# A reloaded tile that lands in the place of its own second norm: adaLN attention and token mixer on one Trainium2 core

## The chip, the cores and the metric

The kernel runs on one core of a Trainium2 chip. Its engines are TensorE (PE in the profile), VectorE (DVE), ScalarE (ACT), GpSimd (POOL) and SyncE (SP), which here issues all DMAs, in the order in which they stand in its queue. Every engine works through its own instructions in order and waits for the others by semaphores.

The metric is the device time of the whole program in microseconds (us). Each line of the profile's views that begins with a time gives it in us from the start of the span.

## The reference

Sequence length 2048, width 1024, 32 heads, 3584 hidden units of the mixer. Cut to what matters here:

```python
x = A_x
mod = (_silu(c) @ w_mod).reshape(c.shape[0], 6, 1, -1)
sa, ca, ga, sb, cb, gb = (mod[:, i] for i in range(6))
h = _layernorm(x) * (1 + ca) + sa
x = x + ga * _A_ref(h, wq, wk, wv, wo, beta)     # attention with memory, then @ wo
h = _layernorm(x) * (1 + cb) + sb                # first norm of the stage below, modulated
x = x + gb * _B_ref(h, w1, b1, w2, b2)           # _B_ref begins with h = _layernorm(h): the second norm
```

`_B_ref` is an MLP over the tokens: second layer norm, `w1` (tokens to 3584), gelu, `w2` back, transposed. So after the attention's output projection each token passes through two layer norms in a row, with a modulation between them, before the token MLP.

## The kernel before

The program has three stages: attention (projections, scores, values, to about 1060 us), the output projection with the two norms (989 to 1213 us, its beginning interleaved with the last heads of the attention), and the token MLP in two large products (from 1214 us to the end). The change lies in the middle stage.

The 2048 tokens are 16 tiles of 128. `product(tt)` (L711) makes the attention's output for one tile: it loads the head outputs (`otr`, L714), splits them into a high and a low part (`ots`; ACT casts, DVE subtracts), loads the tile's rows of x (`x1`, L718), and runs 48 matmuls, 24 for each half of the columns, into a PSUM bank of the tag `pj`, which has two. DVE evicts each half by adding it to x and summing the row (L732). The sum, x1, is stored to `x1d` (L734), since it is needed again much later.

`out_proj(tt)` (L739) then returns three functions. `modulated` (L750) computes the mean, has ACT square the whole tile for the variance (`rstd`, L699; the square is L703, its small operations L705 to L709), and makes two passes on DVE: L754, out of x1 into h2, and L755, in place on h2. `normed` (L757) is the second norm: mean (L759), square on ACT (L703 again, of h2), small operations, and one pass on ACT in place (L762). `paired` (L764) keeps h2 of tiles 0 to 7; when tile k+8 is done, it forms with tile k the seven operands of a Strassen-like product: combinations by DVE (L688 to L691), then for k under 3 seven splits into the tiles `bA` (ACT casts, DVE subtracts, L122 and L125), and for other k stores to `hcd` (L777 to L779).

The order of the tiles is 0, 1, 8, 2, 9, 3, 10, 4, 11, 5, 12, 6, 13, 7, 14, 15. There is one exception: after tile 1 the products of tiles 2 and 3 (`EARLY`) are made at once, while the attention still runs, without their norms. So the products' order is 0, 1, 2, 3, 8, 9, 10, 4, 11, 5, ... When tiles 2 and 3 come up in the order, their x1 is loaded again from `x1d` (L744) and only the norms are made.

Places in SBUF come from pools by tag. `x1` has two places (512 KB each); all sixteen x1 and, before the change, both reloads share them in the order in which they are asked for. `h2` has three. A tile that asks for a place waits, by semaphores, until the last reader of the tile before it in that place is done. A scheduler orders each engine's instructions when the program is built; nothing is ordered by hand around the change, and a different pool use gives a different order on each engine.

When the stage ends, its pools are closed and the first product of the token MLP begins: `prepare` (L798) loads a unit of `w1` (L803) and splits it into seven operands `sp` (casts by ACT, L122), `load_b` (L855) loads the pairs stored in `hcd` back (L858), and `mix` (L828) runs the matmuls (L843).

Of the kernel before, what the change touches and what calls it, by code (L numbers as in the profile page):

```python
# [7 lines left out]
F32 = mybir.dt.float32  # L8
# [9 lines left out]
S, D, H, DH, F = 2048, 1024, 32, 32, 3584  # L18
P = 128
# [27 lines left out]
def attention_and_mlp(ctx, tc, x, wq, wkv, wo, beta, w1, b1, w2, b2, c, wm_a, wm_b, out):  # L47
    nc = tc.nc
    V, A, G, T, SY = nc.vector, nc.scalar, nc.gpsimd, nc.tensor, nc.sync
# [4 lines left out]
    x1d = dram.tile([NT, P, D], F32, name="x1d")  # L54
# [63 lines left out]
    def split(dst, src, hi_eng, lo_eng):  # L118

        hi, lo = dst[:, 0], dst[:, 1]  # L120
        if hi_eng is A:
            A.copy(hi, src)  # L122
        else:
            hi_eng.tensor_copy(hi, src)
        lo_eng.tensor_tensor(lo, src, hi.bitcast(F32), op=ALU.subtract)  # L125
# [541 lines left out]
    w = cw_pool.__enter__()  # L667
# [18 lines left out]
    def t_combos(E, b11, b12, b21, b22, t):  # L686

        E.tensor_tensor(t[:, 0], b12, b11, op=ALU.subtract)  # L688
        E.tensor_tensor(t[:, 1], b22, t[:, 0], op=ALU.subtract)
        E.tensor_tensor(b12, b22, b12, op=ALU.subtract)  # L690
        E.tensor_tensor(t[:, 2], b21, t[:, 1], op=ALU.subtract)  # L691
# [7 lines left out]
    def rstd(src, nm, mv, sq):  # L699

        if sq is None:
            sq = wq_.tile([P, D], BF16, tag="sq", bufs=1, name="sq")
        A.activation(sq, src, AF.Square, bias=nm, accum_out=mv[:, 2:3])  # L703
        v, r0, t = mv[:, 0:1], mv[:, 1:2], mv[:, 2:3]
        A.activation(r0, t, AF.Ln, scale=1.0 / D, bias=eps)  # L705
        A.activation(r0, r0, AF.Exp, scale=-0.5)
        V.tensor_scalar(v, t, -0.5 / D, -0.5 * EPS, op0=ALU.mult, op1=ALU.add)
        V.tensor_scalar(t, v, r0, r0, op0=ALU.mult, op1=ALU.mult)
        V.tensor_scalar(r0, t, 1.5, r0, op0=ALU.add, op1=ALU.mult)  # L709

    def product(tt):  # L711

        r = wr_.tile([P, NK, P], F32, tag="otr", bufs=1, name=f"otr{tt}")
        SY.dma_start(r, oT[:, :, P * tt:P * tt + P].rearrange("g p n -> p g n"))  # L714
        os_ = ws_.tile([P, 2, D], F32R, tag="ots", bufs=2, name=f"ots{tt}")
        split(os_, r.rearrange("p a b -> p (a b)"), A, V)
        x1 = w.tile([P, D], F32, tag="x1", bufs=2, name=f"x1_{tt}")
        SY.dma_start(x1, x[P * tt:P * tt + P])  # L718
        ma = w.tile([P, 8], F32, tag="ma", bufs=2 + len(EARLY), name=f"ma{tt}")
        if tt == 0:  # L720
            for i in range(1, 3):
                gm[i] = w.tile([P, D], F32, name=f"gm{i}")
                spread(gm[i], i)
        for nh in range(2):
            ps = bank("pj", 2, f"po{tt}_{nh}")
            n = 0
            for ct in range(NK):
                for i, j in ((0, 0), (0, 1), (1, 0)):
                    T.matmul(ps, os_[:, i, P * ct:P * ct + P], wop[ct, nh][:, j], start=(n == 0), stop=(n == 3 * NK - 1))  # L729
                    n += 1  # L730
            c0, c1 = 512 * nh, 512 * nh + 512
            V.scalar_tensor_tensor(x1[:, c0:c1], ps, 1.0, x1[:, c0:c1], op0=ALU.mult, op1=ALU.add,  # L732
                                   accum_out=ma[:, 5 + nh:6 + nh])
        SY.dma_start(x1d[tt], x1)  # L734
        return x1, ma

    done = {}

    def out_proj(tt):  # L739

        if tt in done:
            ma = done[tt]
            x1 = w.tile([P, D], F32, tag="x1", bufs=2, name=f"x1r_{tt}")
            SY.dma_start(x1, x1d[tt])  # L744
        else:
            x1, ma = product(tt)
        h2 = w.tile([P, D], F32, tag="h2", bufs=3, name=f"h2_{tt}")
        mb = w.tile([P, 8], F32, tag="mb", bufs=2, name=f"mb{tt}")

        def modulated():  # L750
            nm = ma[:, 4:5]
            V.tensor_scalar(nm, ma[:, 5:6], ma[:, 6:7], -1.0 / D, op0=ALU.add, op1=ALU.mult)
            rstd(x1, nm, ma, h2 if tt == 15 else None)
            V.scalar_tensor_tensor(h2, x1, nm, gm[2], op0=ALU.add, op1=ALU.mult)  # L754
            V.scalar_tensor_tensor(h2, h2, ma[:, 1:2], gm[1], op0=ALU.mult, op1=ALU.add, accum_out=mb[:, 5:6])  # L755

        def normed():  # L757
            nm = mb[:, 4:5]
            V.tensor_scalar_mul(nm, mb[:, 5:6], -1.0 / D)  # L759
            rstd(h2, nm, mb, x1 if tt == 15 else None)  # L760
            V.tensor_scalar_mul(mb[:, 3:4], nm, mb[:, 1:2])
            A.activation(h2, h2, AF.Identity, scale=mb[:, 1:2], bias=mb[:, 3:4])  # L762

        def paired():  # L764
            if tt < 8:
                pair_h[tt] = h2
                return
            k = tt - 8
            first = pair_h.pop(k)
            t = w.tile([P, 3, 512], F32, tag="tc", bufs=1, name=f"tc{k}")  # L770
            t_combos(G if k == 7 else V, first[:, 0:512], first[:, 512:], h2[:, 0:512], h2[:, 512:], t)
            if k < 3:
                src = [first[:, 0:512], t[:, 0], t[:, 1], h2[:, 0:512], first[:, 512:], h2[:, 512:], t[:, 2]]
                for q in range(NPR):
                    split(bA[q][:, k], src[q], A, V)
            else:
                SY.dma_start(hcd[k, :, 0:2], first.rearrange("p (a n) -> p a n", a=2))  # L777
                SY.dma_start(hcd[k, :, 2:4], h2.rearrange("p (a n) -> p a n", a=2))
                SY.dma_start(hcd[k, :, 4:7], t)  # L779

        return modulated, normed, paired

    for tt in [0] + [i for k in range(1, 8) for i in (k, 7 + k)] + [15]:
        rest = out_proj(tt)
        if tt < 15:
            for f in rest:
                f()
        if tt == 1:
            for i in EARLY:
                done[i] = product(i)[1]  # L790
# [256 lines left out]
```

## Time and profile before

| | us |
|---|---|
| median of three runs | 2290.84 (2290.21 to 2291.17) |
| the profiled execution | 2293.52 |
| its span | 2291.7 |
| PE busy | 2214.7 (97%) |
| DVE busy | 1677.2 (73%) |
| ACT busy | 1148.1 (50%) |
| POOL busy | 733.1 (32%) |
| granted clock of PE, mean | 0.988 |

PE is busy almost throughout. In the window from 985 to 1330 us, which holds the middle stage and the start of the MLP, the matmuls of the output projection (`po`, L729) are busy 185.9 us and idle before 16.6 us; all waits of the MLP's first matmuls there come to 2.0 us.

In the timelines a line gives start, duration, engine, source line, operation, out<-in and count; what stands in brackets is the idle time of the engine before it, and who ended that. In the chain of waits a line gives start, duration and the piece of work. `x1`, `x1r` and `x1d` are shown as `x`, `x1r` and `x1d`, `h2` as `h`.

### The profile page before, as it was taken

The numbers are of one execution on the slowest core, as the hardware profiler recorded it, in microseconds if no ns is written. First come the engines' busy times: TensorE is split into PE (matmuls) and PEld (weight loads), VectorE is DVE, ScalarE is ACT, GpSimd is POOL, SyncE is SP. The second block draws the span as 40 slices with busy tenths as digits, with TensorE's granted clock in tenths as the row PEclk, the third lists the DMA queues.
The fourth block names the chain that finished last, engine by engine and source line by source line (L and its number), as shares of the span: only waits on it lengthen the run. The fifth ranks groups of instructions, "written<-read, shape, count | busy, mean of one in ns | idle before, by whom it ended". The sixth has DMA issues, their size and how long they took to land.

```text
span 2291.7 us, 38412 instructions
## 1 busy us (share of the span) xinstructions
PE 2214.7 (97%) x13802; PEld 1903.6 (83%) x13802; DVE 1677.2 (73%) x3798; ACT 1148.1 (50%) x2090; POOL 733.1 (32%) x843
## 2 busy tenths in 40 slices
PE   7999999999999999999799999999999999999999
PEld 6888898888988889987687888888887888888887
DVE  6686677766776777664768565698889787878787
ACT  6476677664665666655555333443334242424232
POOL 5165566564766766644001000023333000000000
PEclk9999999999999999999999999999999999999999
DMA  6656565686566566673366664566557441414133
GB/s 258 201 169 180 144 198 162 180 280 218 165 192 207 169 196 182 202 250 107 114 218 243 238 238 164 192 230 237 207 202 264 173 152 55 152 56 143 55 120 147
DMA packets 172882, 415.72 MB, mean 181 GB/s; under 512 B 17268, under 2 KB 71572, under 8 KB 163732
## 3 DMA queue, kind: packets, MB, share of 16 engines
q1 hardware_dynamic: 172692, 413.27, 54.7%
q8 instruction: 110, 1.80, 0.3%
q14 instruction: 80, 0.66, 0.1%
HBM read 237.28 MB, written 125.06 MB: 158 GB/s over the span
## 4 chain that ended last, share of the span: by engine, by line
PE 77%; DVE 8%; DMA 6%; ACT 3%; POOL 3%; issue 2%; SPq 0%; DVEq 0%; ACTq 0%; POOLq 0%
PE mx L843 42%; PE nps L195 12%; PE qps L203 7%; PE po L729 4%; PE pv L503 3%; POOL ph L489 1%; PE a L474 1%; PE sx L439 1%; DVE ac L850 1%; PE sz L439 1%; DMA x<-in_x_dram 1%; DMA sk<-nt 1%; DVE sp L125 1%; PE rd L411 1%; PE a L477 1%
## 5 line engine op out<-in xcount | busy, mean ns | idle before, releaser
L843 PE MATMUL mx<-bU,sp 128*128 128x512 f32 x2352 | 535.8, 389 | 3.6 <-DVE sp L125 2.1
L843 PEld LDWEIGHTS mx<-bU,sp 128*128 128x128 f32 x2352 | 440.8, 188 | 98.1 <-DVE sp L125 3.2
L195 PE MATMUL nps<-wv,h 128*128 128x256 f32 x3072 | 435.8, 283 | 4.0 <-POOL h L125 3.9
L122 ACT CAST sp<-wr 128x384 fp32r<-128x384 f32 (+2 forms) x408 | 216.8, 545 | 439.4 <-PE mx L843 365.6
L843 PE MATMUL mx<-bA,sp 128*128 128x512 f32 x1764 | 431.5, 389 | 2.0 <-ACT sp L122 1.3
L489 POOL TENSOR_TENSOR ph<-p,ph 128x640 f16<-128x640 f32 x256 | 376.7, 1492 | 152.7 <-ACT ph L487 152.5
L195 PEld LDWEIGHTS nps<-wv,h 128*128 128x128 f32 x3072 | 403.6, 190 | 11.0 <-POOL h L125 5.0
L843 PEld LDWEIGHTS mx<-bA,sp 128*128 128x128 f32 x1764 | 330.8, 188 | 71.6 <-ACT sp L122 2.0
L125 DVE TENSOR_TENSOR sp<-wr,sp 128x384 fp32r<-128x384 f32 (+2 forms) x408 | 260.1, 649 | 31.9 <-ACT sp L122 31.5
L850 DVE TENSOR_TENSOR ac<-mx,ac 128x512 f32<-128x512 f32 x280 | 190.2, 688 | 91.7 <-PE mx L843 91.0
L203 PE MATMUL qps<-h,wq 128*128 128x512 f32 x768 | 200.3, 406 | 2.3 <-DVE pv L506 1.1
L729 PE MATMUL po<-wo,ots 128*128 128x512 f32 x768 | 185.9, 398 | 16.6 <-DVE x L732 14.5
L729 PEld LDWEIGHTS po<-wo,ots 128*128 128x128 f32 x768 | 145.5, 192 | 48.7 <-issue 9.7
L487 ACT CAST ph<-p 128x1280 f16<-128x1280 f32 x128 | 161.2, 1259 | 48.3 <-POOL p L485 47.6
L440 DVE CUSTOM_DVE_ANT_0 sx<-sx,mask 128x128 f32<-128x128 f32 (+1 forms) x256 | 110.1, 430 | 88.5 <-PE sx L439 87.1
L203 PEld LDWEIGHTS qps<-h,wq 128*128 128x128 f32 x768 | 144.1, 194 | 31.5 <-issue 2.8
L843 PE MATMUL mx<-bB,sp 128*128 128x512 f32 x588 | 164.6, 389 | 0.0
L485 POOL TENSOR_SCALAR_AFFINE_SELECT p<-p 128x256 f32<-128x256 f32 x256 | 120.5, 478 | 127.4 <-ACT p L478 68.2
L503 PE MATMUL pv<-vp,ph 128*128 128x97 bf16 (+1 forms) x2560 | 145.1, 203 | 3.3 <-DVE red L510 1.3
L503 PEld LDWEIGHTS <-ph 128*128 128x128 f16 x2560 | 115.9, 99 | 27.9 <-issue 13.1
L843 PEld LDWEIGHTS mx<-bB,sp 128*128 128x128 f32 x588 | 110.4, 188 | 22.9
L850 DVE TENSOR_TENSOR cc<-mx,cc 128x512 f32<-128x512 f32 x140 | 94.3, 684 | 42.5 <-PE mx L843 40.4
(201 smaller groups left out, 3209.2 us busy)
## 6 DMA issues: line engine op xcount, KB each, us to landing
sk<-sg SPq DMA_DIRECT2D x384, 128.0 KB
wr<-in_w_dram SPq DMA_DIRECT2D x28, 1024.0 KB
wr<-in_w_dram SPq DMA_DIRECT2D x32, 768.0 KB
bstu<-ucd SPq DMA_DIRECT2D x28, 768.0 KB
wsp<-wv SPq DMA_DIRECT2D x32, 512.0 KB
rawm<-in_wm_b_dram SPq DMA_DIRECT2D x32, 512.0 KB
wv<-wsp SPq DMA_DIRECT2D x32, 512.0 KB
pcd<-cc SPq DMA_DIRECT2D x14, 1024.0 KB
```

The source lines that it names most:

```text
L122: A.copy(hi, src)
L125: lo_eng.tensor_tensor(lo, src, hi.bitcast(F32), op=ALU.subtract)
L195: T.matmul(ps[:, aa], h[:, j, 128 * tt:128 * tt + 128], wt[:, i, o:o + 256], start=(n == 0), stop=(n >= 6 * NK - 2), skip_group_check=True)
L203: T.matmul(ps, wt[:, i, o:o + 128], h[:, j], start=(k + n == 0), stop=(3 * k + n == 3 * NK - 1))
L440: marks[4 * t + h - LEADS, "V"] = V.tensor_tensor_reduce(o, o, mask[:, 384 - 128 * i:], 1.0, -3.0e38, op0=ALU.add, op1=ALU.max, accum_out= ...
L485: G.affine_select(w, w, pattern=[[0, 2], [1, 128]], compare_op=ALU.is_ge, fill=0.0, base=0, channel_multiplier=-1)
L487: marks[n, "A"] = A.copy(ph[:, 0], p32)
L489: marks[n, "G"] = G.tensor_tensor(ph[:, 1, c], p32[:, c], ph[:, 0, c], op=ALU.subtract)
L503: T.matmul(pv[:, i, 0:w], ph[:, part, o:o + 128], d["vp"][:, j, h, 0:w], start=(n == 0), stop=(n == 19), skip_group_check=True)
L729: T.matmul(ps, os_[:, i, P * ct:P * ct + P], wop[ct, nh][:, j], start=(n == 0), stop=(n == 3 * NK - 1))
L843: T.matmul(ps, ops[q][:, i, P * k:P * k + P], b[:, j], start=(m == 0 and first), stop=(m == 3 * nk - 1), skip_group_check=True)
L850: V.tensor_tensor(d, ps, d, op=ALU.add)
```

## The change

The reload of tiles 2 and 3 no longer asks for a place of the tag `x1`. It goes into the tile's own `h2` place, which `out_proj` asks for anyway; `modulated` then reads and writes the same place in its first pass (L754), and the square of the first norm reads it there too. The number of loads, their size and the passes stay.

```diff
     def out_proj(tt):
 
-        if tt in done:
-            ma = done[tt]
-            x1 = w.tile([P, D], F32, tag="x1", bufs=2, name=f"x1r_{tt}")
-            SY.dma_start(x1, x1d[tt])
-        else:
+        if tt not in done:
             x1, ma = product(tt)
         h2 = w.tile([P, D], F32, tag="h2", bufs=3, name=f"h2_{tt}")
+        if tt in done:
+            x1, ma = h2, done[tt]
+            SY.dma_start(x1, x1d[tt])
         mb = w.tile([P, 8], F32, tag="mb", bufs=2, name=f"mb{tt}")
```

In the program that is built from it, tiles 8, 9, 10, 4, 11, ... take the two places of `x1` in turn with no reload between them. Tile 2's reload asks for the place that tile 8's h2 leaves, tile 3's for the one that tile 9's leaves. The matmuls of the output projection stand in the same order as before; the orders on DVE, ACT and SP differ from the middle of the stage on, and the order of the first matmuls of the MLP differs too. POOL's order is the same.

## The prediction

> **What bounds the kernel now.** I read the page first, then PE's timeline around the changed loop, then the chain of waits there, then the timelines of SyncE's queue (SP), ScalarE (ACT) and VectorE (DVE). The page: TensorE is busy for 97% of the span, and among its groups the output projection has the largest idle time before a matmul, nearly all of it a wait for the eviction that adds x.
>
> ```profile
> span 2291.7 us, 38412 instructions
> L729 PE MATMUL po<-wo,ots 128*128 128x512 f32 x768 | 185.9, 398 | 16.6 <-DVE x L732 14.5
> ```
>
> PE's timeline (start, duration, idle time before) shows where the 14.5 us lie. A tile is 48 matmuls.
>
> ```profile
> 1076.47 20.70 PE L729 MATMUL po<-wo,ots 128*128 128x512 f32 x90
> 1106.44 13.80 PE L729 MATMUL po<-wo,ots 128*128 128x512 f32 x48 [9.27 <-DVE x L732]
> 1121.99 22.02 PE L729 MATMUL po<-wo,ots 128*128 128x512 f32 x96 [1.76 <-DVE x L732]
> 1145.53 22.01 PE L729 MATMUL po<-wo,ots 128*128 128x512 f32 x96 [1.52 <-DVE x L732]
> 1169.03 43.80 PE L729 MATMUL po<-wo,ots 128*128 128x512 f32 x192 [1.49 <-DVE x L732]
> 1214.14 2.87 PE L843 MATMUL mx<-bA,sp 128*128 128x512 f32 x11 [1.31 <-ACT sp L122]
> ```
>
> Tiles run 8, 9, 10, 4, 11, 5, 12, ...; so 1106.44 is tile 4, 1121.99 tile 11 (tile 5 follows at 1133.0, after 48 of the 96), 1145.53 tile 12. Two PSUM banks serve them: tile 4 may start only when tile 10's first half is evicted, and that needs tile 10's x. The chain of waits says why that x came late:
>
> ```profile
> 1099.72 1.13 ACT sq L703 x2
> 1100.88 4.69 DMA x<-in_x_dram
> 1105.59 1.31 DVE x L732 x4
> ...
> 1161.69 6.39 DMA x<-in_x_dram
> ...
> 1202.90 4.52 DMA x<-in_x_dram
> ```
>
> x has two places. Tile 10's x takes the one of tile 9, whose last reader is tile 9's square on ACT; the load leaves as that square ends. So the stage is a loop: square of one tile, load of a later one, eviction, matmuls. SP's queue:
>
> ```profile
> 1078.36 0.33 SPq L718 DMA_DIRECT2D x<-in_x_dram  x1
> ...
> 1094.33 0.32 SPq L744 DMA_DIRECT2D x1r<-x1d  x1
> ...
> 1100.88 0.33 SPq L718 DMA_DIRECT2D x<-in_x_dram  x1
> ...
> 1125.30 0.33 SPq L718 DMA_DIRECT2D x<-in_x_dram  x1
> ...
> 1141.18 0.33 SPq L718 DMA_DIRECT2D x<-in_x_dram  x1
> ...
> 1202.90 0.33 SPq L718 DMA_DIRECT2D x<-in_x_dram  x1
> 1203.51 0.63 SPq L734 DMA_DIRECT2D x1d<-x  x1
> ```
>
> These are the loads of tiles 9, 10, 11, 5 and 15, tile 3's reload and tile 14's store. ACT and DVE in the same stretch:
>
> ```profile
> 1082.57 1.13 ACT L703 ACTIVATE sq<-x1r,ma 128x1024 bf16<-128x1024 f32 x1
> ...
> 1122.56 1.15 ACT L703 ACTIVATE sq<-h,mb 128x1024 bf16<-128x1024 f32 x1 [0.72 <-DVE mb L759]
> ...
> 1124.04 1.13 ACT L703 ACTIVATE sq<-x,ma 128x1024 bf16<-128x1024 f32 x1
> 1125.08 0.19 ACT L703 ACTIVATION_READ_ACCUMULATOR sq<-x,ma 128x1 f32 x1
> ```
>
> ```profile
> 1090.01 1.29 DVE L125 TENSOR_TENSOR bA<-h,bA 128x512 fp32r<-128x512 f32 x2
> ...
> 1098.29 1.23 DVE L125 TENSOR_TENSOR ots<-otr,ots 128x1024 fp32r<-128x1024 f32 x1 [0.32 <-ACT ots L122]
> ...
> 1114.42 0.68 DVE L125 TENSOR_TENSOR bA<-h,bA 128x512 fp32r<-128x512 f32 x1
> ...
> 1116.22 1.28 DVE L754 SCALAR_TENSOR_TENSOR h<-x1r,ma,gm 128x1024 f32<-128x1024 f32 x1
> ...
> 1119.22 1.28 DVE L755 SCALAR_TENSOR_TENSOR h<-h,ma,gm 128x1024 f32<-128x1024 f32 x1
> ...
> 1127.75 0.15 DVE L759 TENSOR_SCALAR mb<-mb 128x1 f32<-128x1 f32 x1
> 1130.22 0.69 DVE L732 SCALAR_TENSOR_TENSOR x<-po,x 128x512 f32<-128x512 f32 x1 [2.32 <-DMA x<-in_x_dram]
> ...
> 1144.69 0.69 DVE L732 SCALAR_TENSOR_TENSOR x<-po,x 128x512 f32<-128x512 f32 x1 [0.54 <-issue]
> ```
>
> **The change part by part.** Nothing is added or dropped: two reloads of 512 KB, the same passes of the same shapes, POOL's order untouched. What moves is where the reload lands.
>
> *The x place that comes free: -9.3 us.* Tile 2's reload no longer sits between tile 8's x and tile 9's. Each load takes the slot of the one before: tile 10's goes where tile 9's stands (1078.36), and its x is there long before 1097. Tile 4 then starts at 1076.47+20.70 = 1097.2, not 1106.44.
>
> *What is late next.* The load that now waits for tile 9's square is tile 4's. That square stands on ACT behind tile 2's second square, as before, and tile 2 begins later: its reload must wait until tile 8's h2 has been read by the split into bA_5 (the second of the two at 1090.01, end 1091.3). Two things pull that in: tile 2's first square (1082.57, 1.13+0.19) no longer precedes tile 8's norm, and an ots split (1.2, as at 1098.29) now stands behind it: about 1088.9. The reload takes between 3.5 us (load 1141.18 to its eviction 1144.69) and 4.7 (1100.88), then square 1.3, first pass 1.3, small ones and one split 1.2: 1096.3 to 1097.5. Next on DVE stands tile 10's second eviction, which PE feeds at 1097.2; then second pass 1.3, ots split 1.2, small 0.3, the two squares 1.5 and 1.3: tile 4's load leaves at about 1103.5, 2.6 later than tile 10's did. It lands at 1107.0 to 1108.2; PE ends tile 4 at 1108.2, so tile 11 hardly waits.
>
> *Tile 3's reload.* In DVE's new order one eviction (0.6), not two, precedes tile 9's second norm, so pair (1, 9) is 0.8 to 2.0 later; its bA_5 split (1114.42, end 1115.1) ends at 1115.9 to 1117.1. Only then does tile 3's reload leave, 22 us after its 1094.33. In before the data waited for DVE; now the chain is in series: reload 3.5, square 1.4, pass 1.3, split 0.6, small 0.5, second pass 1.3, small 0.2, second square 1.5, and behind it on ACT tile 10's square 1.3: 11.6 us. That square ends at 1127.6 to 1128.8 (now 1124.04+1.13+0.19, so 1125.3), and tile 11's load leaves then, not at 1125.30. With 3.5 to 4.9 us to eviction (1125.30 to 1130.22), it comes at 1131.1 to 1133.7, and tile 5 starts 0.8 later (1144.69 to 1145.53): 1131.9 to 1134.5, against 1133.0 now. PE ended tile 11 at 1119.2. The 9.3 us are not saved: they are waited out at tile 5, some 14 us.
>
> *From tile 5 to tile 12: +2.5 us.* Now tile 10's second norm begins at 1127.75, while DVE waits for tile 11's x; in the new order it stands behind both evictions (1.2). From there: second norm with tile 4's square in between 5.5, seven pair operations of 0.6 (two in 1.29 at 1090.01), then DVE's first passes, the split and an ots split 6.0, 0.8 to PE: 17.8 from tile 11's eviction to tile 12, against 1130.22 to 1145.53 = 15.3. With the eviction 0.9 to 3.5 later, tile 12 starts 3.4 to 6.0 us late. I take +4.4, below the middle, since both transfers stand nearly alone, like the 3.5 row. From here on the loop is as it was; the 1.49 stays.
>
> *Handover to the first unit: +1.9 us (0 to 2.5).* In the new order tile 14's store goes out ahead of tile 15's load (now 1202.90 before 1203.51), and tile 7's first pass stands behind one eviction more (0.6). A load behind such stores took 6.39 where this one took 4.52: up to 1.9 more. It delays DVE's passes for tile 14, ACT's square behind them, and the casts of the first weights, on which PE already waits (1.31).
>
> *First two units: +1.5 us (0 to 3.9).* Their matmuls, casts and loads stand in another order. Before has one wait of 1.31 at their start, so there is little to win; I take about one such wait, three as the bound.
>
> On SP, behind the first reload's wait stand tile 11's otr, tile 10's store and tile 4's load: the otr leaves some 0.6 us after it and is needed only at 1108. Behind the second stands tile 11's load, which waits longer for the square.
>
> Sum: 4.4+1.9+1.5 = +7.8 us. The profiled execution took 2293.52 us, 1.8 outside its span of 2291.7, and 2.7 more than the median 2290.84; on the median: 2298.6. Bounds: 3.4 to 12.4, so 2294.2 to 2303.2.
>
> The Trainium skill (Trainium Kernel Development and Optimization, Best Practices) says to double-buffer so that transfers overlap with work, and the change gives that up for two tiles. By that rule alone the price would be two bare reloads, 2 x 3.5 = 7.0 us and 2297.8; no run here shows it yet.
>
> **Rivals.** *Faster: the 9.27 goes and nothing takes its place*, 2281.6. For it: PE has 21 us of work ready between 1097 and 1119 and nothing else to wait for. Against: it needs tile 11's x evicted by 1118.4, so tile 10's square done by 1114.9, ten microseconds ahead of 1125.3; it decides itself by whether that square stands before tile 3's squares on ACT, and it stands behind. 7%.
>
> *No change: the loop has slack where I see none*, tile 5 regains up to 1.1 us, tile 12 starts near 1145.5, and the handover stays: 2290.8 to 2293. For it: PE's waits of 1.5 recur whatever came before. 13%.
>
> *Slower still: the clock.* After the 9.27 us PE ran at half clock; tile 4 took 13.80 us where 48 matmuls take 11.0.
>
> ```profile
> core 0: us, PE busy (x) PEld busy (x) DVE busy (x) ACT busy (x) POOL busy (x), PEclk, DMA share, GB/s
> ...
> 1106.40:1112.00 5.60, 5.56 (x13) 4.43 (x14) 2.50 (x12) 4.44 (x9) 0.00 (x0) 0.50 0.25 97
> ```
>
> The 2.8 us hid under tile 11's wait then, and would hide under tile 12's now; if tile 12 starts cold too, up to 2.8 come on top: 2301.4. 13%. The Trainium skill (TensorE: Matmul & The Clock Gate, Part 1) puts the half clock after one idle window of about 3.4 us; the 0.50 row agrees, and by that rule both new waits would start cold.
>
> **How the numbers follow.** My forecast 67%, the rivals 7, 13 and 13. 0.2%, or 4.6 us, is about what a measurement of this kernel can tell from no change; of the forecast I give 6% to its lower end, under +4.6 us. So slower 0.61+0.13 = 0.74, same 0.13+0.06 = 0.19, faster 0.07. The likeliest one's own range is 2294.2 to 2303.2; with most of the no-change case it becomes 2291.0 to 2303.2.
>
> **What would show it.** Tile 4 starting without a wait near 1097; one wait of 10 us or more at tile 5, with tile 11's load leaving as tile 10's square ends; reloads of tiles 2 and 3 near 1089 and 1116, each followed by its square within 5 us; tile 12 three to six us later than 1145.53. I am wrong if tile 5 waits under 5 us, or if the two new waits together are not more than the old ones.

## The result, and the profile after

The changed kernel takes 2300.94 us (median of 6 runs, 2296.3 to 2304.88); the kernel before, run beside it, takes 2290.95 us (6 runs, 2289.0 to 2294.16). The ratio is 1.0041, 95% interval 1.0028 to 1.0055: 10 us slower, by more than the 0.2% that such a measurement can tell. The profiled execution took 2301.85 us, with a span of 2300.1.

The chain of events is the forecast one. PE's timeline of the changed kernel (start, duration, idle time before, who ended it):

```profile
1075.14 42.46 PE L729 MATMUL po<-wo,ots 128*128 128x512 f32 x186
1131.06 13.59 PE L729 MATMUL po<-wo,ots 128*128 128x512 f32 x48 [13.46 <-DVE x L732]
1147.74 22.01 PE L729 MATMUL po<-wo,ots 128*128 128x512 f32 x96 [3.10 <-DVE x L732]
1171.83 43.80 PE L729 MATMUL po<-wo,ots 128*128 128x512 f32 x192 [2.08 <-DVE ma L707]
1217.24 4.88 PE L842 MATMUL mx<-bA,sp 128*128 128x512 f32 x20 [1.61 <-ACT sp L122]
...
1225.52 4.39 PE L842 MATMUL mx<-bA,sp 128*128 128x512 f32 x18 [1.11 <-ACT cc L847]
...
1257.93 6.00 PE L842 MATMUL mx<-bA,sp 128*128 128x512 f32 x18 [2.12 <-DVE cc L849]
```

The first row now holds tiles 9, 10, 4 and 11 without a gap: the 9.27 us in front of tile 4 are gone. Tile 5 (1131.06) waits 13.46 us, tile 12 (1147.74) 3.10. The table of PE's waits between 985 and 1330 us (in all, times, longest) says the same of the changed kernel,

```profile
PE po L729 <- DVE x L732: 16.6, 2, 13.5
PE mx L842 <- DVE cc L849: 2.1, 1, 2.1
```

and of the kernel before:

```profile
PE po L729 <- DVE x L732: 14.5, 5, 9.3
```

Five waits of 14.5 us became two of 16.6, and the wait before tile 13 (2.08 us, 1.49 before) is now put down to another line of DVE (L707). And a wait has appeared in the MLP (L849), where the change touches nothing.

To compare executions place by place, I count each from the same matmul, tile 9's seventh, which begins PE's first row: 1076.47 in the profiled execution of before, 1075.14 in that of after. Up to there PE, DVE and ACT do the same work in the same order in both kernels; in the thirteen profiled executions of this document that matmul begins anywhere from 1072.0 to 1079.5 us. The start of tile 5 is then 0.6 us earlier than in before (1131.06 - 1075.14 = 55.92 against 1133.0 - 1076.47 = 56.53), tile 12 starts 3.5 later, the projection ends 4.1 later (1171.83 + 43.80), the MLP starts 4.4 later, and the span ends 9.7 later. So 4.1 us are lost in the projection, 0.3 at the handover and 5.3 after 1217 us.

SP's queue of the changed kernel, with tile 2's reload, tile 4's load, tile 3's reload and tile 11's load:

```profile
1087.53 0.32 SPq L746 DMA_DIRECT2D h<-x1d  x1
...
1101.87 0.33 SPq L718 DMA_DIRECT2D x<-in_x_dram  x1
...
1114.78 0.32 SPq L746 DMA_DIRECT2D h<-x1d  x1
...
1126.51 0.33 SPq L718 DMA_DIRECT2D x<-in_x_dram  x1
```

ACT of the changed kernel: a cast for tile 12's product, then tile 3's first square, tile 3's second, tile 10's square:

```profile
1117.64 1.04 ACT L122 CAST ots<-otr 128x1024 fp32r<-128x1024 f32 x1 [2.83 <-PE po L729]
1118.59 1.14 ACT L703 ACTIVATE sq<-h,ma 128x1024 bf16<-128x1024 f32 x1
...
1123.79 1.15 ACT L703 ACTIVATE sq<-h,mb 128x1024 bf16<-128x1024 f32 x1 [3.02 <-DVE mb L758]
...
1125.27 1.13 ACT L703 ACTIVATE sq<-x,ma 128x1024 bf16<-128x1024 f32 x1
1126.30 0.18 ACT L703 ACTIVATION_READ_ACCUMULATOR sq<-x,ma 128x1 f32 x1
```

Tile 10's square ends at 1126.48, and tile 11's load leaves at 1126.51. DVE of the changed kernel in between:

```profile
1116.48 1.28 DVE L753 SCALAR_TENSOR_TENSOR h<-x,ma,gm 128x1024 f32<-128x1024 f32 x1
...
1118.71 1.23 DVE L125 TENSOR_TENSOR ots<-otr,ots 128x1024 fp32r<-128x1024 f32 x1 [0.36 <-ACT ots L122]
...
1119.93 1.27 DVE L753 SCALAR_TENSOR_TENSOR h<-h,ma,gm 128x1024 f32<-128x1024 f32 x1
...
1130.21 0.69 DVE L732 SCALAR_TENSOR_TENSOR x<-po,x 128x512 f32<-128x512 f32 x1 [1.28 <-DMA x<-in_x_dram]
```

Between the start of tile 3's reload (1114.78) and tile 3's square (1118.59) DVE does other work: tile 10's first pass (1116.48), a pair combination, and then a split for the next product (1118.71). It idles 0.36 us. And the square shows no wait of its own: it follows the cast on ACT at once. That will matter below.

The loss after 1217 us: the stretches of the changed kernel around tile 5's start and around the wait at L849 (busy time of PE, weight loads, DVE, ACT, POOL; granted clock; DMA share; GB/s),

```profile
1250.00:1262.00 12.00, 9.65 (x35) 6.90 (x34) 8.35 (x14) 2.80 (x5) 0.00 (x0) 0.88 0.98 362
1131.00:1137.00 6.00, 5.95 (x16) 4.70 (x17) 2.35 (x12) 4.82 (x10) 0.00 (x0) 0.56 0.21 87
```

the former in the kernel before,

```profile
1250.00:1262.00 12.00, 12.00 (x54) 9.95 (x53) 7.23 (x11) 5.23 (x10) 0.00 (x0) 1.00 1.03 399
```

and DVE of the changed kernel there:

```profile
1255.99 1.28 DVE L895 SCALAR_TENSOR_TENSOR xb<-gb,b2s,xb 128x1024 f32<-128x1024 f32 x1 [3.34 <-DMA xb<-x1d]
1257.19 0.68 DVE L849 TENSOR_TENSOR cc<-mx,cc 128x512 f32<-128x512 f32 x1
```

DVE stands 3.34 us at a pass that needs a row tile from memory, while the DMA engines are full (share 0.98; they are as full in before, where in this stretch no eviction stands right behind such a row). The eviction PE waits for stands behind that pass. PE does 35 matmuls in these 12 us instead of 54, some of them at half the granted clock (0.88 over the stretch).

### The profile page after: what moved, and what is told of

Read it like the earlier page. It is cut to its first block, busy times and chain, and to the rows that moved or that the text cites. A ratio compares the mean times of both kernels' runs of the same rounds, so it can differ in the third digit from the quotient of the medians.

```text
span 2300.1 us, 38410 instructions
## 1 busy us (share of the span) xinstructions
PE 2216.6 (96%) x13802; PEld 1905.0 (83%) x13802; DVE 1676.9 (73%) x3798; ACT 1149.3 (50%) x2090; POOL 738.1 (32%) x843
## 4 chain that ended last, share of the span: by engine, by line
PE 81%; DVE 5%; DMA 5%; ACT 4%; POOL 3%; issue 2%; SPq 0%; DVEq 0%; POOLq 0%; ACTq 0%
PE mx L842 44%; PE nps L195 12%; PE qps L203 7%; PE po L729 6%; PE pv L503 3%; DMA sk<-nt 2%; POOL ph L489 1%; PE a L474 1%; PE sx L439 1%; PE sz L439 1%; PE rd L411 1%; PE a L477 1%; ACT ph L487 1%; DMA x<-in_x_dram 1%; PE up L421 1%
## 5 line engine op out<-in xcount | busy, mean ns | idle before, releaser
L849 DVE TENSOR_TENSOR ac<-mx,ac 128x512 f32<-128x512 f32 x280 | 189.3, 685 | 93.9 <-PE mx L842 93.3
L729 PE MATMUL po<-wo,ots 128*128 128x512 f32 x768 | 187.5, 401 | 21.0 <-DVE x L732 16.6
L688 POOL TENSOR_TENSOR tu<-cc 128x512 f32<-128x512 f32 x14 | 21.3, 1523 | 340.2 <-DVE cc L978 273.3
```

What stands on the lines that cost most here:

```text
L849: V.tensor_tensor(d, ps, d, op=ALU.add)
```

## The experiments

All times are ratios to the kernel before, run on the same chip. The right columns are read from the profiled executions, one of each kernel, counted from tile 9's seventh matmul, in us against before: the end of the projection, the end of the span, and what lies between.

| kernel | ratio (95%) | us | end of projection | end of span | between |
|---|---|---|---|---|---|
| the change | 1.0041 (1.0028 to 1.0055) | +10.0 | +4.1 | +9.7 | +5.6 |
| e1, tile 3 alone | 1.0033 (1.0021 to 1.0045) | +7.4 | +2.7 | +7.9 | +5.2 |
| e2, tile 2 alone | 1.0019 (1.0010 to 1.0028) | +5.0 | +2.0 | +5.2 | +3.2 |
| e3, reload twice | 1.0045 (1.0029 to 1.0061) | +9.3 | +8.1 | +12.6 | +4.5 |
| e4, rows late | 1.0024 (1.0015 to 1.0033) | +4.9 | +4.3 | +5.8 | +1.5 |
| e7, no reload | 1.0024 (1.0016 to 1.0033) | +5.2 | +7.0 | +6.2 | -0.8 |
| e5, change with new order | 0.9957 (0.9944 to 0.9970) | -10.2 | -10.4 | -10.5 | -0.1 |
| e6, before with new order | 0.9956 (0.9944 to 0.9967) | -11.2 | -10.3 | -10.1 | +0.2 |
| e8, e5 with rows late | 0.9956 (0.9944 to 0.9968) | -9.7 | -11.2 | -11.2 | 0.0 |
| e9, change, 10 before 3 | 0.9994 (0.9983 to 1.0004) | -1.1 | -2.8 | -0.3 | +2.5 |
| e10, before, 10 before 3 | 0.9996 (0.9986 to 1.0007) | -0.2 | -1.4 | -0.4 | +1.0 |
| e11, before, rows late | 0.9994 (0.9983 to 1.0004) | -0.5 | +1.5 | +0.7 | -0.8 |

**The parts alone.** e1 gives only tile 3 the new place, e2 only tile 2 (`tt == 2` in both lines):

```diff
-        if tt not in done:
+        if tt in done and tt != 3:
+            ma = done[tt]
+            x1 = w.tile([P, D], F32, tag="x1", bufs=2, name=f"x1r_{tt}")
+            SY.dma_start(x1, x1d[tt])
+        elif tt not in done:
             x1, ma = product(tt)
...
-        if tt in done:
+        if tt == 3:
```

> Only tile 3's reload goes into its h2 place; tile 2's keeps an x1 place as before. Theory (the loop of squares and loads sets the stage; a reload in an h2 place adds its transfer in series): tile 10's x takes the place that tile 2 leaves after its first pass, so the wait before tile 4 shrinks from 9.3 to 2 us or less, a wait of about 11 us stands before tile 5, tile 12 starts within 1 us of before, and the whole is 2 to 5 us slower than before. Rival (each reload in h2 costs the same half): 5 us slower with a wait of about 5 at both tiles. Rival (the stage decides nothing, the first units of the token MLP do): 7 us or more slower, as the full change minus its stage.

> Only tile 2's reload goes into its h2 place; tile 3's keeps an x1 place. Theory: tile 3's reload now follows tile 8 in its x1 place and tile 10's load still waits for tile 9's square, so the wait before tile 4 stays at 9 to 11 us, nothing is gained there, tile 12 starts about 2 us late, and the whole is 3 to 6 us slower. Rival (freed x1 places are what counts, and one is freed here): the wait before tile 4 goes to under 3 us and the whole is not slower.

PE's timeline of e1, then of e2:

```profile
1130.08 13.79 PE L729 MATMUL po<-wo,ots 128*128 128x512 f32 x48 [9.72 <-DVE x L732]
```

```profile
1102.36 12.77 PE L729 MATMUL po<-wo,ots 128*128 128x512 f32 x48 [9.64 <-DVE x L732]
...
1142.01 23.65 PE L729 MATMUL po<-wo,ots 128*128 128x512 f32 x96 [2.09 <-DVE x L732]
```

With tile 3 alone the long wait stands at tile 5, with tile 2 alone at tile 4: each kernel has one wait of 9.6 to 9.7 us, and it goes where the reading of x is late. Neither part is a gain by itself. Tile 3's projection behaves as my theory had it (2 to 5 us); its total, 7.4, is the rival's, since 5.2 us are lost in the MLP. Tile 2's part came as expected in its wait and its total (5.0 us), but tile 12 starts only 0.9 us late, not 2.

**The reload doubled, and taken out.** e3 issues each reload twice, into the same place. e7 drops it and lets the norm read a modulation row that lies in SBUF:

```diff
             x1, ma = h2, done[tt]
             SY.dma_start(x1, x1d[tt])
+            SY.dma_start(x1, x1d[tt])
```

```diff
-            x1, ma = h2, done[tt]
-            SY.dma_start(x1, x1d[tt])
+            x1, ma = gm[1], done[tt]
```

> The changed kernel with each of the two reloads issued twice in a row into the same place, the second waiting for the first; nothing else differs in what is computed. Theory (the transfer stands in series in the loop): the wait before tile 5 grows by 3 to 4 us from 13.5, tile 12 and everything behind it come 2.5 to 3.5 us later than in the changed kernel, which is 12 to 13 us over before. Rival (the transfer is hidden, the loss is the order of the instructions): no difference from the changed kernel, within 1.5 us.

> The changed kernel without the two reloads: the first norm of tiles 2 and 3 reads a tile that lies in SBUF anyway (one of the modulation rows), so tiles 2 and 3 are not computed, all passes stay. Theory of the reload in series (prediction: 3.5 us from reload to square, then the rest): the square of tile 3 comes 3.5 us earlier, tile 11's load leaves 3 us or more earlier, tile 5 waits 10 us or less instead of 13.5, and the time is at most 5 us over the kernel before (ratio 1.002 or less). Rival (the order alone holds tile 10's square; the passes for tile 9's pair and the split for the next product stand ahead of tile 3's first pass whatever the data do): tile 5 still waits 12 to 15 us and the time is that of the changed kernel, 7 to 11 us over the kernel before (ratio 1.003 to 1.005).

PE's timeline of e3:

```profile
1133.92 12.99 PE L729 MATMUL po<-wo,ots 128*128 128x512 f32 x48 [14.56 <-DVE x L732]
```

its ACT at tile 3's square, and the same square in e1:

```profile
1122.39 1.15 ACT L703 ACTIVATE sq<-h,ma 128x1024 bf16<-128x1024 f32 x1 [1.44 <-DMA h<-x1d]
```

```profile
1116.26 1.15 ACT L703 ACTIVATE sq<-h,ma 128x1024 bf16<-128x1024 f32 x1 [2.91 <-DMA h<-x1d]
```

and, of e7, first PE, then ACT (the first squares of tiles 3 and 10), then DVE:

```profile
1129.93 12.97 PE L729 MATMUL po<-wo,ots 128*128 128x512 f32 x48 [13.69 <-DVE x L732]
1145.40 22.05 PE L729 MATMUL po<-wo,ots 128*128 128x512 f32 x96 [2.51 <-DVE x L732]
1171.83 45.16 PE L729 MATMUL po<-wo,ots 128*128 128x512 f32 x192 [4.37 <-DVE x L732]
```

```profile
1106.55 1.13 ACT L703 ACTIVATE sq<-gm,ma 128x1024 bf16<-128x1024 f32 x1
...
1124.29 1.13 ACT L703 ACTIVATE sq<-x,ma 128x1024 bf16<-128x1024 f32 x1
```

```profile
1116.24 1.28 DVE L752 SCALAR_TENSOR_TENSOR h<-gm,ma,gm 128x1024 f32<-128x1024 f32 x1
```

A reload of 512 KB more makes tile 5 start 3.2 us later than in the changed kernel (1133.92 - 1074.85 = 59.07 against 55.92), nearly the whole transfer, and tile 3's square now waits 1.44 us for it. That is what the theory expected; the time, +9.3, is what the rival expected, and the times alone do not part e3 from the change. But the reload taken away gains nothing at tile 5: 13.69 us of wait, and tile 10's square 50.67 us after the common matmul (1124.29 - 1073.62), against 50.13 in the changed kernel. For the changed kernel the theory of a reload in series falls here, and the rival holds at tile 5. Tile 3's square is ready 18 us ahead of tile 10's, but its first pass still waits for tile 9's pair on DVE (1116.24), and then comes the work that in the changed kernel was done under the reload. The transfer and DVE's own list are about equally long: one more transfer shows, one fewer does not. (Without the reload the scheduler also moved tile 3's first square ahead of two casts, so e7 is not the same order less one transfer; the 4.37 us at tile 13 belong to its own order.) The changed kernel's own trace agrees. In e3 the second copy, which waits for the first, leaves 3.25 us after it (1119.21 against 1115.96), so by this estimate tile 3's reload is there at about 1118.0 in the changed kernel, while the cast holds ACT until 1118.6. It is not so everywhere: in e1, where only tile 3's reload moved, the square does wait 2.91 us for the reload. e7's total, +5.2, lies between what the two expected, for a reason that neither had: e7 loses nothing in the MLP.

**The order.** e5 (on the change) and e6 (on the kernel before) take tile 9 ahead of tile 2, tile 10 ahead of tile 3, and so on, so that the norms of 2 and 3 no longer hold them up:

```diff
-    for tt in [0] + [i for k in range(1, 8) for i in (k, 7 + k)] + [15]:
+    for tt in [0, 1, 8, 9, 2, 10, 3, 11, 4, 12, 5, 13, 6, 14, 7, 15]:
```

> The changed kernel, with the tiles taken in the order 0, 1, 8, 9, 2, 10, 3, 11, 4, 12, 5, 13, ... instead of 0, 1, 8, 2, 9, 3, 10, 4, 11, 5, ...: the norms of tiles 2 and 3 stand behind the product and the first square of tiles 9 and 10, all work is kept. My theory: the 13.5 us at tile 5 are made by tile 10's square, which stands on ACT behind tile 3's squares and holds the x place for the next load; with tile 9's and tile 10's squares ahead of those, no tile of the stage waits more than 3 us, the projection ends 8 to 10 us earlier than in the kernel before, and the time is 8 to 10 us under it (ratio 0.9956 to 0.9965). Rival (the stage is bound by DVE and ACT, and a wait removed at one tile comes back at the next): one wait of 8 us or more stays in the stage, and the time is within 4 us of the changed kernel's (ratio 1.002 to 1.006).

> The kernel before, with the same order 0, 1, 8, 9, 2, 10, 3, 11, 4, 12, ... and the reloads in the tag x1 as before. My theory: in the kernel before, too, what holds the loads is the order of the squares on ACT, not the place that the reloads take; so the 9.3 us at tile 4 go here as well, spread over smaller waits: 7 to 10 us under the kernel before (ratio 0.9956 to 0.997). Rival (the reload's place in the tag x1 is what makes the 9.3 us): a wait of 8 us or more stays, and the time is within 3 us of the kernel before (ratio 0.9987 to 1.0013).

PE, SP (tile 4's load, tile 3's reload) and ACT (tile 10's square, tile 3's) in e5:

```profile
1073.46 53.34 PE L729 MATMUL po<-wo,ots 128*128 128x512 f32 x234
1131.74 67.70 PE L729 MATMUL po<-wo,ots 128*128 128x512 f32 x288 [4.94 <-DVE x L732]
```

```profile
1107.70 0.33 SPq L718 DMA_DIRECT2D x<-in_x_dram  x1
1108.27 0.32 SPq L746 DMA_DIRECT2D h<-x1d  x1
```

```profile
1106.39 1.14 ACT L703 ACTIVATE sq<-x,ma 128x1024 bf16<-128x1024 f32 x1
...
1117.28 1.13 ACT L703 ACTIVATE sq<-h,ma 128x1024 bf16<-128x1024 f32 x1
```

PE in e6:

```profile
1115.64 88.65 PE L729 MATMUL po<-wo,ots 128*128 128x512 f32 x384 [4.60 <-DVE x L732]
```

Both are 10 to 11 us faster than the kernel before and some 20 faster than the change. The projection ends 10.4 and 10.3 us earlier, a little more than the 7 to 10 asked for; "no tile waits more than 3 us" did not come, since one wait of 4.9 and one of 4.6 are left. With this order the place of the reload is worth nothing that can be measured: the ratios of e5 and e6 differ by 0.0001, with intervals of 0.0013 to either side. So the 9.3 us of the kernel before and the 13.5 of the change have one cause, the order of the readers of x, and the change only moved it from tile 9's readers to tile 10's.

e9 and e10 exchange only tiles 10 and 3 (`[0, 1, 8, 2, 9, 10, 3, 4, 11, 5, 12, ...]`), in the change and in the kernel before:

> The changed kernel with one pair of tiles exchanged: 0, 1, 8, 2, 9, 10, 3, 4, 11, 5, 12, ..., so that only tile 10 comes ahead of tile 3; tile 9 stays behind tile 2, and all work is kept. My theory: tile 4's and tile 11's starts stay as in the changed kernel (no wait), and of the 13.5 us at tile 5 at least half go, since tile 11's load no longer waits for tile 3's norm; the projection ends 3 us or more earlier than in the changed kernel, and the time is 0 to 8 us under the kernel before (ratio 0.9965 to 1.000). Rival (what holds tile 11's x is tile 9's lateness, inherited from tile 2): tile 5 still waits 10 us or more and the time is 6 to 11 us over the kernel before (ratio 1.0025 to 1.005).

> The kernel before with the same exchange, 0, 1, 8, 2, 9, 10, 3, 4, ...; the reloads stay in the tag x1. Tile 10's x then takes the place of tile 2's reload instead of tile 9's x. Theory (the time is set by which tile's readers a load has to wait for, and the reload's place as such is worth little): tile 4's wait falls from 9.3 us to under 5, later waits of 1 to 4 us appear, and the time is 0 to 8 us under the kernel before, within 4 us of e9. Rival (the reload in the tag x1 costs the 9.3 us whatever the order): tile 4 still waits 8 us or more, and the time is within 2 us of the kernel before.

PE's timeline of e9, then PE's and DVE's (tile 10's first pass) and SP's (tile 4's load) of e10:

```profile
1121.52 12.70 PE L729 MATMUL po<-wo,ots 128*128 128x512 f32 x48 [4.96 <-DVE x L732]
...
1162.32 45.39 PE L729 MATMUL po<-wo,ots 128*128 128x512 f32 x192 [4.11 <-DVE x L732]
```

```profile
1101.76 11.16 PE L729 MATMUL po<-wo,ots 128*128 128x512 f32 x48 [1.57 <-DVE x L732]
1124.48 89.96 PE L729 MATMUL po<-wo,ots 128*128 128x512 f32 x384 [11.56 <-DVE x L732]
```

```profile
1117.61 1.28 DVE L754 SCALAR_TENSOR_TENSOR h<-x,ma,gm 128x1024 f32<-128x1024 f32 x1
```

```profile
1118.92 0.33 SPq L718 DMA_DIRECT2D x<-in_x_dram  x1
```

In e9 tile 5's wait falls from 13.46 to 4.96, as my theory asked, and the kernel makes up the 10 us that the change had cost; it is not faster than before by a measurable amount, since 4.11 us appear at tile 13 and 2.5 in the MLP. The 4.96 us that stay at tile 5 are waited for tile 10's first pass: it ends at 1116.43, and tile 11's load leaves at 1116.46. In e10 the wait leaves tile 4, and stands with 11.56 us at tile 11 in place of the small ones I expected; the total, within 0.1% of before, fits the rival as well as the theory. The reason is visible, and the same as in e9: here the last reader of tile 10's x is not the square but the first pass on DVE, which stands behind tile 9's pair and ends at 1118.89; tile 4's load leaves at 1118.92.

**The MLP's start.** In e4 the bias rows of the first units are asked for later, in the changed kernel; in e11 in the kernel before; e8 adds it to e5:

```diff
-            for tt in range(row, min(row + (0, 1, 2)[min(g, 2)], NT)):
+            for tt in range(row, min(row + (0, 2)[g > 2], NT)):
```

> The changed kernel with the sixteen bias rows of the token MLP (load of x1d, one pass on DVE, store) begun from the fourth unit on, two a unit, not from the second on. Theory (about 5 us of the loss lie at 1247 to 1270 us, where DVE waits 3.3 us for such a row's load in a full DMA queue while an eviction stands behind it): these 5 us mostly go, the whole is 4 to 6 us over before, and PE's wait of 2.1 us there is gone. Rival (the loads of the first units crowd the queue with or without the rows): 9 to 10 us over before, as the changed kernel.

> The kernel before with the bias rows asked for later, as e4 did to the changed kernel. Theory (in the changed kernel the row's load stood in front of an eviction only because the first units came late and in another order): here PE has no wait of 1 us or more at the eviction near 1250 us as it stands, so the edit is worth nothing: ratio 0.9987 to 1.0013. Rival (asking later is better in any order): 3 to 5 us under the kernel before (ratio 0.9978 to 0.9987), which would make e4's gain no part of what the change costs.

> The changed kernel with the order of e5, and the early bias rows of the MLP's first units asked for later, as in e4. Theory: two separate costs add up, so this is 2 to 5 us under e5, as e4 was 3 to 5 under the changed kernel: 10 to 14 us under the kernel before (ratio 0.994 to 0.9956), and PE does not wait for the eviction at 1250 us. Rival (the 2.1 us wait there came from how late the stage ended, so with the stage 13 us earlier it does not occur anyway): the time is within 1.5 us of e5's.

e4 takes the 2.12 us at L849 away: DVE makes the first row's pass at 1259.71, behind the evictions that it stood ahead of in the change. The projection ends where it ends in the change (+4.3 us against +4.1). PE's timeline from tile 12 on:

```profile
1149.31 68.22 PE L729 MATMUL po<-wo,ots 128*128 128x512 f32 x288 [3.10 <-DVE x L732]
```

The loss after the projection falls from 5.6 to 1.5 us in the profiles. The medians of e4 and of the change lie 0.0017 apart with intervals that meet, so the times alone would not settle it. On the kernel before the edit is worth nothing (e11), as expected, and on e5 nothing either (e8): the expected addition missed, and the rival's time held, though the lateness that it gave as the reason is not the cause, as follows. The row's load hurts only in the order of the first units that the change happened to bring. That order is the same in the change, e1, e2, e3 and e4, and all five lose 1.5 to 5.6 us after the projection. e7 and e11 have the order of the kernel before, and lose nothing there, though e7 comes 7.0 us late. So it is not lateness that costs in the MLP, but the order.

Counted matmul by matmul from the MLP's first one (a unit has 84), the traces part this loss. Each of the five kernels loses 2.0 to 2.1 us up to the 150th matmul and 0.5 from the 175th to the 252nd. Between these, where the row's load stands, the change loses 4.1 us, e1 and e2 0.8 to 0.9, e3 2.0 and e4 nothing. e7 and e11 lose nothing in any of these stretches. What follows goes both ways (-1.4 us in the change, +1.4 in e1) and stays unexplained. So the order by itself costs 2.5 us, with the rows or without; which of its moved instructions do it was not tried.

A reload with a place of its own, or a third place in the tag x1, was not tried.

## Why the prediction was right, point by point

It said 2298.6 us (2291.0 to 2303.2); 2300.94 came, slower by 10.0 us against +7.8.

*The x place that comes free* and *What is late next*: right. Tile 4 has no wait. With the executions put on one count (+1.33), tile 2's reload left at 1088.9 as forecast, tile 4's load at 1103.2 (1103.5), and tile 11 did not wait.

*Tile 3's reload*: right in every time. It left at 1116.1 (1115.9 to 1117.1), tile 11's load at 1127.8 (1127.6 to 1128.8), tile 5 started at 1132.4 (1131.9 to 1134.5), the wait was 13.46 (14). The reason given was right in one half only. That tile 10's square stands behind tile 3's is the cause of most of the wait; e5 and e9 show it (in e9 4.96 us are left). That "now the chain is in series" with the reload is not, since e7 without the reload waits as long: DVE's work filled the transfer. One piece was left out of that series, the cast for tile 12 that stood ahead of tile 3's square until PE had done tile 11. That the sum came out all the same is luck: the cast ended about when the transfer did, 3.8 us after the reload left, where 3.5 were taken.

*From tile 5 to tile 12*: taken +4.4, measured +3.5 at tile 12 and +4.1 at the end of the projection. The sentence "from here on the loop is as it was" missed 0.6 us: the 1.49 became 2.08.

*Handover to the first unit*: taken +1.9, measured +0.3. The store did go out ahead of tile 15's load, which took 5.44 us in the chain of waits in place of 4.52, but PE waited 1.61 in place of 1.31:

```profile
1207.04 5.44 DMA x<-in_x_dram
```

*First two units*: taken +1.5, at most 3.9; measured +6.1 in their 168 matmuls, and +5.3 by the end of the span (0.6 more in the third unit, 1.4 gained later). This is the term of the sum that was mis-sized, and by it the total is over the forecast. I bounded it by three of the waits that were there, about 1.3 each. What came was another kind: a load in a full queue in front of an eviction (2.12 us), the half clock after it (18 matmuls in 6.00 us in place of 4.39), and 2 us of smaller losses that all kernels with this order share. The errors of the three terms, -0.3, -1.6 and +3.8, leave 1.9 us: 9.7 by the profiles against 7.8. So it is partly luck that the total came so near: one term passed its own bound, and the other two made up for half of that.

The rivals. *Faster* needed tile 10's square ahead of tile 3's, and it was not. e9 makes just that exchange and comes to -1.1 us; e5, which also takes tile 9 ahead of tile 2, comes to -10.2, against the 9.2 that the rival gave. *No change* did not come. *Slower still, the clock*: tile 5 started near half clock (0.56 in its first 6 us, 13.59 us for 48 matmuls), and the time that it lost so went into tile 12's wait. Tile 12 itself ran at full clock (96 matmuls in 22.01 us), so this rival's 2.8 us did not come where it put them. In e4 they did come there: after the same wait of 3.10 us the matmuls from tile 12 on are 2.6 us slower; but the wait of 2.08 us before tile 13 is gone in exchange, and the projection ends only 0.2 us later. The sentence on the Trainium skill's clock page (TensorE: Matmul & The Clock Gate, Part 1) held for the first of the two waits and not for the second, which at 3.10 us is shorter than its window. The sentence on the Trainium skill's Best Practices (Trainium Kernel Development and Optimization) gave 2297.8, which is near the result for the wrong reason: with the right order, giving up the second buffer costs nothing that can be measured (e5 against e6).

## What to carry to other kernels

When a place is shared in turn, a load leaves with the last reader of the tile before it; so look for where that reader stands in its engine's queue, behind whose work, before looking at places and transfers. Freeing a place moves the wait to the next late reader, here from 9.3 us at one tile to 13.5 at another; putting the readers first, by the order of the tiles, removed both for 10 us. And any edit that lets the scheduler reorder may cost elsewhere: over half of this loss (5.6 of 9.7 us) lay after the stage that the change touches.

## What the runs showed of the hardware

Waits of PE between 2 and 3 us cost a further 1.6 us in some cases and nothing in others. A row of e11:

```profile
1117.66 23.64 PE L729 MATMUL po<-wo,ots 128*128 128x512 f32 x96 [2.90 <-DVE x L732]
```

96 matmuls take 22.02 us at full speed and 192 take 43.80; for 288 that gives 65.6, an estimate. So waits in the projection of 2.09 (e2), 2.47 (e3, 192 matmuls in 45.41 behind it) and 2.90 us were followed by 1.6 us of loss, and 2.08 (the change) and 2.51 (e7) by none. A wait of 3.10 us at tile 12 was followed by none in the change and by 2.6 in e4 (288 matmuls in 68.22). Those up to 1.84 us (e9) cost 0.1 at most, and those of 4.1 to 5.0 us cost 1.3 to 2.1. The length of the wait alone does not decide.

The granted clock shows what does. In these traces it changes in steps of 3.41 us: each slow stretch from tile 9 on lasts 3.41, 6.83, 10.24 or 13.65 us. Here are the step that holds most of the 3.10-us wait and the step behind it, in the change and then in e4 (busy time of PE, weight loads, DVE, ACT, POOL; granted clock; DMA share; GB/s):

```profile
1143.10:1146.51 3.41, 1.55 (x7) 0.94 (x5) 3.38 (x5) 1.04 (x1) 0.00 (x0) 1.00 0.44 154
1146.51:1149.92 3.41, 2.18 (x10) 1.84 (x11) 2.10 (x8) 1.58 (x4) 0.00 (x0) 1.00 0.47 133
```

```profile
1144.77:1148.18 3.41, 1.44 (x7) 0.86 (x5) 3.30 (x5) 1.04 (x1) 0.00 (x0) 1.00 0.39 143
1148.18:1151.60 3.42, 2.29 (x6) 1.84 (x7) 1.99 (x8) 1.70 (x4) 0.00 (x0) 0.50 0.51 150
```

PE idles 1.86 us of the first step in the change, and 1.97 in e4 (the ends of matmuls are modelled in the profile). In all thirteen traces, between 1085 and 1290 us, every step at full clock with 1.97 us of idle time or more is followed by one at half clock (21 steps), and no step with 1.87 or less is. So a wait of 2 to 3 us is dear or free by how the edge of a step divides it, and a wholly idle step is not needed. The Trainium skill (TensorE: Matmul & The Clock Gate, Part 1) says that the activity window runs freely, some 3.4 us long; the steps of 3.41 us, whose edges fall at a different place of the wait in each execution, agree with that.
